# Attention, gated convolution and spatial gating on one core: q and k loads with an earliest time, a mask added by TensorE, and bits found by ScalarE

## The chip, the cores and the metric

The kernel runs on one core of a Trainium2 chip. The metric is the device time of one execution in microseconds (us). The times shown are the median of three runs and, beside it, one execution that was profiled.

## What is computed

The reference chains three parts on 4 batches of 576 positions, in float32 at the end:

```python
# q, k, v: (4, 8, 576, 64); window 64, causal
scores = q @ k.T / 8;  mask = (0 <= rel) & (rel < 64)
attn = softmax(where(mask, scores, -1e9)) @ v          # per head, then heads side by side: x (4, 576, 512)
h = relu(x @ w_in)                                     # w_in (512, 1024)
conv = sum over k of conv_w[k] * h shifted by k - 1    # 3 taps along the positions
y = (h * sigmoid(conv)) @ w_out                        # w_out (1024, 512)
h2 = relu(y @ w2_in); u, v2 = the halves of h2
vn = layer norm of v2;  vs = w_spatial @ vn + b        # mixes the positions
out = (u * vs) @ w2_out
```

The matrices of weights come as 64-bit floats; the kernel reads them as pairs of 32-bit words and makes 32-bit floats of them by integer operations.

## The kernel before, in words

**Attention.** The 36 blocks of 64 queries are taken in pairs, 18 rounds in all (`rec_round`, p = 0 to 17). A round multiplies q with k for both blocks and all heads into two PSUM tiles s, one per head half (L537, 32 products). VectorE adds the mask and takes the row's extreme in one fused instruction per head pair (L553, four per half), writing masked scores into the SBUF tile sm. ScalarE takes exponentials in place with the sum beside them (L562, eight per round), then follow the reciprocal (L570, L571), the normalisation (L578 on ScalarE or L582), transposes by TensorE (L592), copies to pts, the products with v (L618) and the split of the result into a rounded high part and a low part (xc, L285 and L306). The tag s has two buffers and vw, the values, three.

**Loads.** Batch 0's q and k come in five pieces (`rec_load_first`, L454) that TensorE transposes (L489). Batches 1 to 3 come in eight loads each, four of q and four of k (`rec_load_qk`, L466), in pieces of 128 bytes, which VectorE then transposes in blocks of 32 (L503). Values come by L477. All go through one queue, SyncE's, in the order of the list.

**Weights.** `rec_conv` loads one 128x512 tile of 64-bit words (raw, two buffers), scales the high words (L285, wt), takes the low words' upper bits (u1, `low_bits`, L410) and the sign (u2, `sign_bits`, L416) and joins them (u3, L422). 28 such tiles are converted: eight of w_in, eight of w_out, eight of w2_in, four of w2_out. Then each is split into a high and a low part.

**Stage 1** takes the positions in eight chunks of 288 (two a batch). Chunk 0 needs rounds 0 to 2, chunk 1 rounds 3 and 4. `rec_g1` makes one block of 128 columns of h: 12 products of 128x290 (L710 to L712), relu (L301), three taps (L733, L738), tanh (L749), gate (L753) and a split. `rec_g2` makes y (L777 to L779) and stores it to DRAM (L802). **Stage 2** loads y again and makes v, u, the spatial mixing (L1053 to L1059), the gate (L1067, L1070) and the last products (L1106 to L1108).

**What sets the order.** The kernel records operations with a rank, the engines that may do them, their cost, and what they read, write and hold (`Plan.op`). `Plan.emit` then plays them through as a list scheduler and writes out the instructions in the order in which it started them; each engine works through its own in that order. A free engine takes the ready operation of the lowest rank. Where several engines may do one, it takes the one with the least of its waiting work and cost times a bias: by planner time t the bias is BIAS1 below TE1, BIAS2 below TE2, BIAS after that; ScalarE's is 1. The loads are operations on the planner's engine "D": the queue is held 0.45 (ISSUE) for each, the wires for their cost, and the next can be issued without a look at the wires. An operation is ready once all it reads is there and the buffer that it takes over is free; the queue isn't held idle for a rank that lies far ahead.

The ranks come from the constants of PLAN: TA is the rank of round 0, TR the step of the first three rounds, TL and T_G make the chunks' starts, RD and LEAD place the later rounds, QL and QL1 the loads of q and k before their round, VL those of the values, WI, WIS, WO, WOS and W2 the weights, LD a load before its conversion.

Of the kernel before, what the change touches and what calls it, by code (L numbers as in the profile page):

```python
# [15 lines left out]
PSUM = bass.MemoryType.PSUM  # L16
NEG = -8.0e9
BIG = 3.0e38
EXP_SHIFT = 2.0 ** -112

PLAN = {
    "BP": 2.148,
    "BP1": 0.05,
    "BP2": 15.503,
    "BV": 0.462,
    "BV1": 0.753,
    "BV2": 4.229,
    "CS": 2.842,
    "CW": 4.897,
    "CWL": -1.999,  # L30
    "DC": 1.72,
    "G2": 7.85,
    "LAT": 0.209,
    "LD": 0.07,
    "LEAD": -0.623,
    "PORT": 1.851,
    "QK": 0.74,
    "QL": -0.201,
    "QL1": -1.324,
    "QV": -0.054,  # L40
    "RD": 5.317,
    "RS": 1.023,
    "SW": 4.365,
    "TA": -1.408,
    "TE1": 1.82,
    "TE2": 574.465,
    "TL": 1.208,
    "TR": 0.83,
    "VL": -0.489,
    "W2": 13.512,  # L50
    "WI": 1.844,
    "WIS": -0.265,
    "WO": -0.591,
    "WOS": 2.232,
}
LAT = PLAN["LAT"]
HOLD, ISSUE = 0.25, 0.45
BIAS = {"V": PLAN["BV"], "P": PLAN["BP"]}
# [26 lines left out]
class Plan:  # L85
# [4 lines left out]
    def __init__(self):  # L90
        self.rows, self.bufs, self.ops = {}, [], []
        self.writer, self.readers = {}, {}
        self.port, self.issues = set(), {}

    def buf(self, key, n, make):
        return Buf(self, key, n, make)

    def op(self, rank, engs, fn, r=(), w=(), b=(), after=(), port=False, issues=1):


        i = len(self.ops)
        if port:
            self.port.add(i)
        self.issues[i] = issues
        deps = set(after)
# [12 lines left out]
        for x in b:  # L118
            x.users.append(i)
        deps.discard(i)  # L120
        self.ops.append([rank, engs, fn, deps, b])
        return i

    def emit(self):
# [19 lines left out]
        for i in range(n):  # L144
            if not left[i]:
                heapq.heappush(events, (0.0, 0, i))
        port_free = wire = 0.0
        order = []
        t = 0.0
        while events:  # L150
            t = events[0][0]
            while events and events[0][0] <= t + 1e-9:
                _, kind, i = heapq.heappop(events)
                if kind == 0:
                    rank, opt = ops[i][0], ops[i][1]
# [12 lines left out]
            for e in engs:  # L168
                while ready[e] and free[e] <= t + 1e-9:
# [44 lines left out]
def tile_attention_convglu_spatial(  # L214
# [46 lines left out]
    ident = const.tile([P, P], F, name="ident")  # L261
    masks = [const.tile([P, P], F, name=f"mask{j}") for j in range(3)]
    cw = const.tile([P, 3, KF], F, name="cw")
# [91 lines left out]
    def setup_masks(e):  # L355


        for mk_, first in zip(masks, ((False, False), (True, False), (False, True))):
            for h in range(2):
# [15 lines left out]
    op(-9.0, {"A": 1.6}, setup_table, w=["zero1"])  # L375
    op(-8.0, {"P": 3.0}, setup_masks, w=["masks"])

# [29 lines left out]

    def low_bits(u, raw):
# [51 lines left out]
    def rec_load_qk(b, rank):  # L460

        for nm, src, dst in (("q", q, qT), ("k", k, kT)):
            for g in range(4):
                def ld(e, src=src, dst=dst, g=g):
# [44 lines left out]
    def x_pieces(blocks):  # L509
# [10 lines left out]
        return out_  # L520

    x_keys = {qc: [] for qc in range(NQ)}

    def rec_round(p, rank):
# [5 lines left out]
        st = mk(at, [P, 3, 2, HP], F, "st", "st", 3)  # L530

        def mm_s(e):
# [9 lines left out]
        op(  # L542
            rank, {"T": 1.1}, mm_s,
            r=[("q", b, i) for b, i in blocks] + [("k", b, k0 + o) for (b, _), k0 in zip(blocks, k0s) for o in range(2)],
            w=[("s", p, h) for h in range(2)], b=pss + [qT[b] for b in bs] + [kT[b] for b in bs],
        )
        firsts = [i == 0 for _, i in blocks]
        mask = masks[1 if firsts[0] else 2 if firsts[1] else 0]
# [45 lines left out]
        for h in range(2):  # L594
            op(rank + 1 * rs + 0.1 * h, {"V": 1.46}, mx(h), r=[("s", p, h), "masks"], w=[("sm", p, h)], b=[pss[h], sm[h], st])
            op(rank + 2 * rs + 0.1 * h, {"A": 1.9}, ex(h), r=[("sm", p, h)], w=[("ex", p, h)], b=[sm[h], st])
            if p < first_rounds:
# [42 lines left out]
    def rec_conv(rank, load, n, issues=1, lead=PLAN["LD"]):  # L640
# [14 lines left out]
        def u1(e):  # L655
            low_bits(u(), raw())

# [541 lines left out]
```

## Time and profile before

| | us |
|---|---|
| median of 3 runs | 548.48 (547.16 to 550.54) |
| profiled execution, its own time | 549.49 |
| its span, first to last instruction | 547.7 |
| TensorE busy in the span | 508.4 |
| VectorE, ScalarE, GpSimd busy | 345.1, 324.4, 4.3 |
| mean granted clock of TensorE (1.0 is 2.4 GHz) | 0.956 |

The span is what the trace covers; the profiled execution's own time has 1.8 us around it. A start in a timeline counts from the span's start. Instructions of one engine overlap a little in the trace, so the time from one start to the next tells what an instruction costs its engine. In the timeline of SyncE's queue the second number is the time that the issue took, for as many transfers as "x" says. The DMA share is the mean busy share of 16 engines and can pass 1 where packets overlap.

### The profile page before, as it was taken

The page shows a single profiled execution, that of the slowest core. Times are in us where ns is not written, and L with a number is a line of the kernel's source. Part 1 is how long each engine was busy: PE and PEld are TensorE (multiplying, and loading weights), DVE is VectorE, ACT ScalarE, POOL GpSimd, SP SyncE. Part 2 cuts the span into 40 slices and gives each one's busy share as a digit, 9 for nine tenths or more (in the row PEclk, how much of TensorE's full clock was granted, in tenths as well). Part 3 has the DMA queues.
Part 4 walks back from the last instruction along what each step waited for, and adds up shares of the span by engine and source line. Part 5 has one row for each costly group of instructions (what it writes and reads, how often), then busy time and mean ns, then how long its engine had stood idle before and what let it go on. Part 6 is the DMA issues. An engine that isn't in the chain of part 4 may idle for free.

```text
span 547.7 us, 11063 instructions
## 1 busy us (share of the span) xinstructions
PE 508.4 (93%) x4198; PEld 472.7 (86%) x4198; DVE 345.1 (63%) x1045; ACT 324.4 (59%) x920; POOL 4.3 (1%) x34
## 2 busy tenths in 40 slices
PE   5745967999999999999999999999999999999997
PEld 5634857899988999999999998898899889988996
DVE  2547768999977989777676634986506740572160
ACT  4875879988959899678785524653322442233221
POOL 3000000000000000000000000000000000000000
PEclk9765788999998999999999999999999999999999
DMA  9999997655996746224216682560105011202003
GB/s 181 173 145 178 147 184 209 190 162 148 208 151 183 226 117 181 68 61 143 69 45 196 215 303 93 166 208 4 59 20 172 1 63 35 87 1 78 1 0 97
DMA packets 131993, 68.05 MB, mean 124 GB/s; under 512 B 105740, under 2 KB 118308, under 8 KB 131940
## 3 DMA queue, kind: packets, MB, share of 16 engines
q1 hardware_dynamic: 131940, 67.35, 51.5%
q8 instruction: 33, 0.54, 0.4%
q14 instruction: 20, 0.16, 0.1%
HBM read 48.98 MB, written 18.35 MB: 123 GB/s over the span
## 4 chain that ended last, share of the span: by engine, by line
PE 80%; DMA 7%; SPq 5%; ACT 3%; DVE 3%; issue 1%; ACTq 0%
PE y L777 6%; PE h L710 5%; PE h L711 5%; PE y L779 5%; PE h L712 5%; PE y L778 5%; DMA vw<-in_v_dram 3%; PE pv L618 3%; PE sps L1053 3%; PE sps L1055 3%; PE sps L1054 3%; PE ops L1108 3%; PE vps L930 3%; PE ops L1107 3%; PE ops L1106 3%; PE vps L929 3%
## 5 line engine op out<-in xcount | busy, mean ns | idle before, releaser
L710 PE MATMUL h<-xc,wi 128*128 128x290 f32 x256 | 79.7, 311 | 2.1 <-ACT hs L301 2.1
L777 PE MATMUL y<-g,wo 128*128 128x288 f32 x256 | 78.4, 306 | 0.8 <-DVE ys L795 0.8
L712 PE MATMUL h<-xc,wi 128*128 128x290 f32 x256 | 77.2, 301 | 0.0
L711 PE MATMUL h<-xc,wi 128*128 128x290 f32 x256 | 77.1, 301 | 0.0
L779 PE MATMUL y<-g,wo 128*128 128x288 f32 x256 | 76.1, 297 | 0.0
L778 PE MATMUL y<-g,wo 128*128 128x288 f32 x256 | 75.9, 296 | 0.0
L738 DVE SCALAR_TENSOR_TENSOR cv<-hs,cw,cv 128x288 f32<-128x288 f32 x128 | 64.5, 512 | 15.9 <-ACT cv L733 14.7
L1067 DVE TENSOR_TENSOR gr<-sps,bb 128x288 f32<-128x288 f32 x32 | 14.5, 454 | 71.9 <-PE sps L1059 71.9
L562 ACT ACTIVATE sm<-sm,st 128x128 f32<-128x128 f32 x144 | 55.7, 391 | 2.2 <-DVE st L553 2.2
L710 PEld LDWEIGHTS h<-xc,wi 128*128 128x128 f32 x256 | 49.9, 195 | 3.8 <-ACT hs L301 2.9
L777 PEld LDWEIGHTS y<-g,wo 128*128 128x128 f32 x256 | 48.5, 189 | 2.7 <-DVE ys L795 1.1
L711 PEld LDWEIGHTS h<-xc,wi 128*128 128x128 f32 x256 | 49.9, 195 | 0.0
L712 PEld LDWEIGHTS h<-xc,wi 128*128 128x128 f32 x256 | 49.6, 194 | 0.1
L779 PEld LDWEIGHTS y<-g,wo 128*128 128x128 f32 x256 | 48.7, 190 | 0.0
L778 PEld LDWEIGHTS y<-g,wo 128*128 128x128 f32 x256 | 48.6, 190 | 0.0
L578 ACT ACTIVATE sm<-sm,st 128x128 f32<-128x128 f32 x132 | 41.1, 393 | 1.0 <-DVE st L571 0.8
L285 ACT ACTIVATE gd<-gr 128x288 fp32r<-128x288 f32 (+1 forms) x32 | 13.4, 418 | 47.2 <-DVE gr L1070 47.2
L553 DVE CUSTOM_DVE_ANT_0 sm<-s,mask 128x128 f32<-128x128 f32 x144 | 32.3, 286 | 10.9 <-PE s L537 10.9
L989 PE MATMUL ups<-yt,w2i 128*128 128x288 f32 x128 | 37.9, 296 | 0.0
L990 PE MATMUL ups<-yt,w2i 128*128 128x288 f32 x128 | 37.9, 296 | 0.0
L991 PE MATMUL ups<-yt,w2i 128*128 128x288 f32 x128 | 37.9, 296 | 0.0
L618 PE MATMUL pv<-pts,vw 128*64 128x64 f32 x576 | 25.8, 250 | 12.5 <-DMA vw<-in_v_dram 9.4
(147 smaller groups left out, 1240.5 us busy)
## 6 DMA issues: line engine op xcount, KB each, us to landing
yd<-ys SPq DMA_DIRECT2D x32, 288.0 KB, 3.0
yt<-yd SPq DMA_DIRECT2D x32, 288.0 KB, 4.3
vw<-in_v_dram SPq DMA_DIRECT2D x32, 256.0 KB, 4.0
raw<-in_moe_w_out_dram SPq DMA_DIRECT2D x12, 512.0 KB, 3.9
raw<-in_moe_w_in_dram SPq DMA_DIRECT2D x16, 256.0 KB, 5.3
raw<-in_moe_w_in_dram SPq DMA_DIRECT2D x8, 512.0 KB, 5.0
w2i<-w2d SPq DMA_DIRECT2D x8, 512.0 KB, 6.1
out_dram<-osb SPq DMA_DIRECT2D x15, 256.0 KB, 2.0
```

The source lines that it names most:

```text
L562: nc.scalar.activation(out=sm[h]()[:, hp, :], in_=sm[h]()[:, hp, :], func=ACTF.Exp, scale=-1.0, bias=st()[:, 0, h, hp:hp + 1], accum_out=s ...
L578: nc.scalar.activation(out=sm[h]()[:, hp, :], in_=sm[h]()[:, hp, :], func=ACTF.Copy, scale=st()[:, 2, h, hp:hp + 1])
L618: mm(psv()[h * W:h * W + W, hp, j * W:j * W + W], vas[j]()[:, hp + HP * h, :], pts[h]()[:, hp, j * W:j * W + W], start=True, stop=True,)
L710: mm(hps(), wh, xh, start=(kk == 0), stop=False)
L711: mm(hps(), wh, xl, start=False, stop=False)
L712: mm(hps(), wl, xh, start=False, stop=(kk == KD - 1))
L738: return lambda e: nc.vector.scalar_tensor_tensor(out=cv(), in0=h[:, o + j:o + j + CH], scalar=cw[:, j, f:f + 1], in1=cv(), op0=ALU.mult, ...
L777: mm(yps(), wt[:, 0], gt[:, 0, :], start=(kk == 0), stop=False)
L778: mm(yps(), wt[:, 0], gt[:, 1, :], start=False, stop=False)
L779: mm(yps(), wt[:, 1], gt[:, 0, :], start=False, stop=(kk == KF - 1))
L989: mm(ups(), wt[:, 0], yt[b][0]()[:, kk, o], start=(kk == 0), stop=False)
L990: mm(ups(), wt[:, 0], yt[b][1]()[:, kk, o], start=False, stop=False)
```

## The change

1. Loads of q and k of batches 1 to 3 get an earliest planner time, `at`, equal to their rank, and a cost of 2.5 in place of 1.8. In the planner a DMA queue now also stays taken until the wires are no more than DEPTH = 6 behind, and ISSUE is 0.5.
2. In rounds 0 to 5 TensorE puts the mask into both score tiles first: a product of the identity and the mask, 128 columns by 512, in fp32r, and the scores are added to it in PSUM. VectorE then takes the maximum of a half in one reduction and multiplies it by -1/8 in a small second instruction; the exponentials read the scores from PSUM. So the score tiles are held until the exponentials are done, and sm is first written by these. The masks are built in a tile of tag wu and copied, with the identity, to fp32r tiles by VectorE (`put_masks`). NEG becomes -2**33.
3. u1 of `rec_conv` may go to VectorE (at 0.05 more) or to ScalarE (at its cost of a 128x512 instruction from SBUF): a copy with scale 2**-13 and bias 2**-14 - 0.5 that writes 16-bit integers.
4. All constants of PLAN but BP1, DC and LAT change, among them the biases: for VectorE 0.753, 4.229, 0.462 become 3.844, 3.449, 1.729 and for GpSimd 0.05, 15.503, 2.148 become 0.05, 3.023, 0.615, and TE2, from which on the last of the three holds, 574.465 becomes 183.169. So any operation may change its place in the order, and some their engine.

```diff
-NEG = -8.0e9
+NEG = -(2.0 ** 33)
...
-    "LEAD": -0.623,
+    "LEAD": 1.709,
-    "QL": -0.201,
-    "QL1": -1.324,
+    "QL": -0.104,
+    "QL1": -4.718,
-    "RD": 5.317,
+    "RD": 1.962,
-    "TA": -1.408,
-    "TE1": 1.82,
-    "TE2": 574.465,
-    "TL": 1.208,
-    "TR": 0.83,
-    "VL": -0.489,
-    "W2": 13.512,
-    "WI": 1.844,
-    "WIS": -0.265,
-    "WO": -0.591,
-    "WOS": 2.232,
+    "TA": -0.261,
+    "TE1": 1.949,
+    "TE2": 183.169,
+    "TL": 0.206,
+    "TR": 6.98,
+    "VL": -18.824,
+    "W2": 83.412,
+    "WI": 0.394,
+    "WIS": -7.725,
+    "WO": 0.771,
+    "WOS": 1.466,
...
-HOLD, ISSUE = 0.25, 0.45
+HOLD, ISSUE, DEPTH = 0.25, 0.5, 6.0
...
-                heapq.heappush(events, (0.0, 0, i))
+                heapq.heappush(events, (max(0.0, self.at.get(i, 0.0)), 0, i))
...
-                            heapq.heappush(events, (t, 0, j))
+                            heapq.heappush(events, (max(t, self.at.get(j, 0.0)), 0, j))
...
-                        free[e] = t + ISSUE * self.issues[i]
+                        free[e] = max(t + ISSUE * self.issues[i], wire - DEPTH)
...
+    mf = mk(p2, [P, 3, P], F, "wu", "mf", 1)
+
+    def put_masks(e):
+        for j in range(3):
+            nc.vector.tensor_copy(out=masks_r[j], in_=mf()[:, j])
+        nc.vector.tensor_copy(out=ident_r, in_=ident)
+    op(-8.0, {"P": 3.0}, setup_masks, w=["masks_f"], b=[mf])
+    op(-7.0, {"V": 0.6}, put_masks, r=["masks_f", "ident"], w=["masks", "masks_r"], b=[mf])
...
+        if e == "A":
+            nc.scalar.activation(
+                out=halves(u)[:, :, 0], in_=halves(raw.rearrange("p c w -> p (c w)"))[:, 0::2, 1],
+                func=ACTF.Copy, scale=2.0 ** -13, bias=2.0 ** -14 - 0.5,
+            )
+            return
...
-                op(rank + 0.1 * g, {"D": 1.8}, ld, w=[(nm, b, "ld", g)], b=[dst[b]])
+                op(rank + 0.1 * g, {"D": 2.5}, ld, w=[(nm, b, "ld", g)], b=[dst[b]], at=rank)
...
+    EARLY = 6
...
+            if early:
+                for h in range(2):
+                    mm(pss[h](), ident_r, masks_r[which].unsqueeze(1).to_broadcast([P, HP, P]), start=True, stop=False)
...
-                            kT[b]()[rows, hp, k0s[j] * W:k0s[j] * W + P], start=True, stop=True,
+                            kT[b]()[rows, hp, k0s[j] * W:k0s[j] * W + P], start=not early,
+                            stop=not early or hp == HP - 1,
...
+                if early:
+                    m = st()[:, 0, h]
+                    nc.vector.tensor_reduce(out=m, in_=pss[h](), axis=mybir.AxisListType.X, op=ALU.max)
+                    nc.vector.tensor_scalar(out=m, in0=m, scalar1=-scale, scalar2=None, op0=ALU.mult)
+                    return
...
+                    src = pss[h] if early else sm[h]
                     nc.scalar.activation(
-                        out=sm[h]()[:, hp, :], in_=sm[h]()[:, hp, :], func=ACTF.Exp, scale=-1.0,
+                        out=sm[h]()[:, hp, :], in_=src()[:, hp, :], func=ACTF.Exp, scale=scale if early else -1.0,
...
+                r=[("sm", p, h)], w=[("ex", p, h)], b=[sm[h], st] + [pss[h]] * early,
...
-        op(rank, {"V": c_ts(n)}, u1, r=[(key, "raw")], w=[(key, "u1")], b=[raw, u], port=True)
+        op(rank, {"V": c_ts(n) + 0.05, "A": c_act(n, False)}, u1, r=[(key, "raw")], w=[(key, "u1")], b=[raw, u], port=True)
```

## Rows read from the trace of the kernel before

**Rows 1.** Page, section 1: busy us (share of the span) xinstructions, each engine

```profile
PE 508.4 (93%) x4198; PEld 472.7 (86%) x4198; DVE 345.1 (63%) x1045; ACT 324.4 (59%) x920; POOL 4.3 (1%) x34
```

**Rows 2.** View of stretches: stretch, length, busy us of each engine, clock, DMA share, GB/s

```profile
7.00:57.10 50.10, 28.03 (x326) 21.94 (x325) 28.27 (x128) 36.27 (x125) 0.00 (x0) 0.66 1.15 173
0.00:57.10 57.10, 33.66 (x353) 27.57 (x354) 29.10 (x133) 37.76 (x127) 4.34 (x34) 0.71 1.09 170
57.10:88.60 31.50, 23.75 (x258) 21.94 (x256) 23.56 (x77) 26.15 (x83) 0.00 (x0) 0.83 1.08 174
88.60:117.00 28.40, 26.31 (x241) 24.63 (x234) 27.80 (x59) 25.43 (x63) 0.00 (x0) 1.00 0.65 191
117.00:544.50 427.50, 424.72 (x3357) 398.59 (x3356) 264.67 (x778) 234.66 (x651) 0.00 (x0) 1.00 0.39 110
```

**Rows 3.** Timeline of TensorE: start us, us, what, [idle before <-releaser]

```profile
43.96 0.66 PE L489 MATMUL tr<-ident,qk 64*128 64x64 f32 x4 [2.78 <-DMA qk<-in_q_dram]
...
53.35 1.76 PE L618 MATMUL pv<-pts,vw 128*64 128x64 f32 x28 [0.72 <-DMA vw<-in_v_dram]
...
57.15 0.59 PE L710 MATMUL h<-xc,wi 128*128 128x290 f32 x1
...
88.66 0.40 PE L710 MATMUL h<-xc,wi 128*128 128x290 f32 x1
```

**Rows 4.** Timeline of SyncE's queue: start us, us in the queue's issue, what

```profile
17.66 1.41 SPq L466 DMA_DIRECT2D qT<-in_q_dram  x1
...
27.11 2.92 SPq L676 DMA_DIRECT2D raw<-in_moe_w_in_dram  x2
30.07 0.60 SPq L466 DMA_DIRECT2D qT<-in_q_dram  x1
...
39.04 2.85 SPq L454 DMA_DIRECT2D qk<-in_q_dram  x2
...
46.03 4.42 SPq L477 DMA_DIRECT2D vw<-in_v_dram  x3
...
52.34 0.60 SPq L466 DMA_DIRECT2D qT<-in_q_dram  x1
...
66.13 2.58 SPq L676 DMA_DIRECT2D raw<-in_moe_w_in_dram  x2
...
70.04 2.80 SPq L466 DMA_DIRECT2D qT<-in_q_dram  x1
...
75.72 2.17 SPq L676 DMA_DIRECT2D raw<-in_moe_w_in_dram  x2
```

**Rows 5.** Timeline of VectorE, same columns

```profile
18.86 0.29 DVE L553 CUSTOM_DVE_ANT_0 sm<-s,mask 128x128 f32<-128x128 f32 x1 [3.31 <-PE s L537]
...
20.55 0.46 DVE L410 TENSOR_SCALAR wu<-raw 128x512 uint16<-128x512 uint16 x1
20.90 0.45 DVE L416 TENSOR_SCALAR wu<-raw 128x512 uint16<-128x512 uint16 x1
...
36.83 0.68 DVE L306 TENSOR_TENSOR xc<-pv,xc 128x512 fp32r<-128x512 f32 x1
37.45 0.29 DVE L553 CUSTOM_DVE_ANT_0 sm<-s,mask 128x128 f32<-128x128 f32 x1
```

**Rows 6.** Timeline of ScalarE

```profile
21.01 0.67 ACT L285 ACTIVATE wt<-raw 128x512 f32<-128x512 f32 x1
21.58 0.39 ACT L562 ACTIVATE sm<-sm,st 128x128 f32<-128x128 f32 x1
...
24.66 0.57 ACT L285 ACTIVATE qT<-tr 128x512 f32<-128x512 f32 x1
```

**Rows 7.** Timeline of TensorE in the last stage

```profile
534.00 0.40 PE L1107 MATMUL ops<-w2o,gd 128*128 128x512 f32 x1
534.24 0.39 PE L1108 MATMUL ops<-w2o,gd 128*128 128x512 f32 x1
```

**Rows 8.** Timeline of GpSimd

```profile
1.02 0.29 POOL masks.py:199 TENSOR_SCALAR_AFFINE_SELECT ident<-ident 128x128 f32<-128x128 f32 x1
```

More of the change, by code (lines that the diff above doesn't have):

```diff
@@ L21 @@
 PLAN = {
-    "BP": 2.148,
+    "BP": 0.615,
     "BP1": 0.05,
[L24 to L30, printed above, removed]
+    "BP2": 3.023,
+    "BV": 1.729,
+    "BV1": 3.844,
+    "BV2": 3.449,
+    "CS": 2.677,
+    "CW": -2.142,
+    "CWL": 0.708,
     "DC": 1.72,
-    "G2": 7.85,
+    "G2": 7.067,
     "LAT": 0.209,
-    "LD": 0.07,
-    "LEAD": -0.623,
-    "PORT": 1.851,
-    "QK": 0.74,
-    "QL": -0.201,
-    "QL1": -1.324,
-    "QV": -0.054,
-    "RD": 5.317,
-    "RS": 1.023,
-    "SW": 4.365,
-    "TA": -1.408,
-    "TE1": 1.82,
-    "TE2": 574.465,
-    "TL": 1.208,
-    "TR": 0.83,
-    "VL": -0.489,
-    "W2": 13.512,
-    "WI": 1.844,
-    "WIS": -0.265,
-    "WO": -0.591,
-    "WOS": 2.232,
+    "LD": -0.554,
+    "LEAD": 1.709,
+    "PORT": 0.519,
+    "QK": 0.218,
+    "QL": -0.104,
+    "QL1": -4.718,
+    "QV": -0.674,
+    "RD": 1.962,
+    "RS": 2.062,
+    "SW": 1.562,
+    "TA": -0.261,
[9 more added lines that the diff above has]
+    "WOS": 1.466,
 }
 LAT = PLAN["LAT"]
-HOLD, ISSUE = 0.25, 0.45
+HOLD, ISSUE, DEPTH = 0.25, 0.5, 6.0
 BIAS = {"V": PLAN["BV"], "P": PLAN["BP"]}
@@ L92, in __init__, with op @@
         self.writer, self.readers = {}, {}
-        self.port, self.issues = set(), {}
+        self.port, self.issues, self.at = set(), {}, {}
     def buf(self, key, n, make):
         return Buf(self, key, n, make)
-    def op(self, rank, engs, fn, r=(), w=(), b=(), after=(), port=False, issues=1):
+    def op(self, rank, engs, fn, r=(), w=(), b=(), after=(), port=False, issues=1, at=0.0):
         i = len(self.ops)
@@ L104, in op @@
         self.issues[i] = issues
+        self.at[i] = at
         deps = set(after)
@@ L261, in tile_attention_convglu_spatial @@
     ident = const.tile([P, P], F, name="ident")
-    masks = [const.tile([P, P], F, name=f"mask{j}") for j in range(3)]
+    masks_r = [const.tile([P, P], R, name=f"mask{j}") for j in range(3)]
+    masks = [x_.bitcast(F) for x_ in masks_r]
+    ident_r = const.tile([P, P], R, name="ident_r")
     cw = const.tile([P, 3, KF], F, name="cw")
@@ L355, in setup_masks @@
     def setup_masks(e):
-        for mk_, first in zip(masks, ((False, False), (True, False), (False, True))):
+        for mk_, first in zip([mf()[:, j] for j in range(3)], ((False, False), (True, False), (False, True))):
             for h in range(2):
@@ L375, in tile_attention_convglu_spatial @@
     op(-9.0, {"A": 1.6}, setup_table, w=["zero1"])
-    op(-8.0, {"P": 3.0}, setup_masks, w=["masks"])
+    mf = mk(p2, [P, 3, P], F, "wu", "mf", 1)
[5 more added lines that the diff above has]
+    op(-7.0, {"V": 0.6}, put_masks, r=["masks_f", "ident"], w=["masks", "masks_r"], b=[mf])
     def setup_ones(e):
@@ L406, in halves, with low_bits @@
         return x_.bitcast(H16).rearrange("p (c w) -> p c w", w=2)
-    def low_bits(u, raw):
+    def low_bits(u, raw, e="V"):
+        if e == "A":
[4 more added lines that the diff above has]
+            return
         nc.vector.tensor_scalar(
@@ L530, in rec_round @@
         st = mk(at, [P, 3, 2, HP], F, "st", "st", 3)
+        firsts = [i == 0 for _, i in blocks]
+        which = 1 if firsts[0] else 2 if firsts[1] else 0
+        mask = masks[which]
+        early = p < EARLY
         def mm_s(e):
+            if early:
+                for h in range(2):
+                    mm(pss[h](), ident_r, masks_r[which].unsqueeze(1).to_broadcast([P, HP, P]), start=True, stop=False)
             for hp in range(HP):
@@ L542, in rec_round @@
         op(
-            rank, {"T": 1.1}, mm_s,
-            r=[("q", b, i) for b, i in blocks] + [("k", b, k0 + o) for (b, _), k0 in zip(blocks, k0s) for o in range(2)],
+            rank, {"T": 1.75 if early else 1.1}, mm_s,
+            r=["masks_r"] * early + [("q", b, i) for b, i in blocks] + [("k", b, k0 + o) for (b, _), k0 in zip(blocks, k0s) for o in range(2)],
             w=[("s", p, h) for h in range(2)], b=pss + [qT[b] for b in bs] + [kT[b] for b in bs],
         )
-        firsts = [i == 0 for _, i in blocks]
-        mask = masks[1 if firsts[0] else 2 if firsts[1] else 0]
         def mx(h):
             def f(e):
+                if early:
[3 more added lines that the diff above has]
+                    return
                 for hp in range(HP):
@@ L594, in rec_round @@
         for h in range(2):
-            op(rank + 1 * rs + 0.1 * h, {"V": 1.46}, mx(h), r=[("s", p, h), "masks"], w=[("sm", p, h)], b=[pss[h], sm[h], st])
-            op(rank + 2 * rs + 0.1 * h, {"A": 1.9}, ex(h), r=[("sm", p, h)], w=[("ex", p, h)], b=[sm[h], st])
+            kept = [sm[h], st] if not early else [st]
+            op(
+                rank + 1 * rs + 0.1 * h, {"V": 0.85 if early else 1.46}, mx(h),
+                r=[("s", p, h), "masks"], w=[("sm", p, h)], b=[pss[h]] + kept,
+            )
+            op(
+                rank + 2 * rs + 0.1 * h, {"A": 1.75 if early else 1.9}, ex(h),
+                r=[("sm", p, h)], w=[("ex", p, h)], b=[sm[h], st] + [pss[h]] * early,
+            )
             if p < first_rounds:
@@ L655, in u1 @@
         def u1(e):
-            low_bits(u(), raw())
+            low_bits(u(), raw(), e)
         def u2(e):
```

## The prediction

> **What bounds the kernel now.** I read the page's busy shares first: TensorE is busy 508.4 of 547.7 us [rows 1], so at most 39 us of standing still can go, and whatever a slow clock costs, and the question is where they lie. The stretches of the span answer it [rows 2]. From 117 to 544.5 us TensorE works 424.7 of 427.5 us at granted clock 1.00 (2.4 GHz), and 3.2 us remain behind its last product: that part gives back no more than 2.8 us. The loss lies ahead. Up to 57.1 us TensorE is busy 33.7 us at a mean clock of 0.71 (1.0 is 2.4 GHz, 0.5 is 1.2), up to 88.6 us 23.8 of 31.5 at 0.83, and from there to 117 us 26.3 of 28.4 at 1.00. Counted at the full level, busy time times clock, the first two stretches hold 23.9 and 19.7 us of work, so 33 and 12 us are lost there, by waiting and by the slow clock.
>
> What TensorE waits for is in its order of time [rows 3]: the last piece of batch 0's q (to 43.96), values of the third round (to 53.35), and only then the first product of stage 1 at 57.15; the eighth block of stage 1 begins at 88.66. Both waits end with a transfer, so next comes the order of SyncE's queue [rows 4]. It starts eight loads of batch 1 from 17.66 to 27.11 and from 30.07 to 39.04, 9.4 and 9.0 us, and only behind them the last piece of batch 0 (39.04) and the values of round three (46.03). Eight loads of batch 2 follow, six from 52.34 to 66.13 and two from 70.04 to 75.72, 19.5 us, ahead of the last block of w_in. One such load holds the queue 2.3 us; the DMA share of 1.09 and 1.08 [rows 2] says that the wires are full, so that is transfer and not issue alone. VectorE and ScalarE are the limit behind that: ScalarE is busy 37.8 of the first 57.1 us, and from 88.6 to 117 VectorE is busy 27.8 of 28.4.
>
> **The loads held back.** In the old list nothing keeps batch 1 and 2 from being planned as soon as the planner's queue is free; there a load costs it 0.45 us, so it sees no jam. Now they have an earliest planner time. By the new constants I work out 27.2 for batch 1, 91.1 for batch 2 and 134.9 for batch 3 (the rank of their first round plus 0.1). Batch 0's last piece has no such time; ahead of it by rank stand eight other q and k loads, one of conv_w, two of w_in and three of v, 17.1 units of wire, which with the new limit of 6 are issued by about 11. So it passes batch 1, and so do the values of round three once their buffers are free. This gives the order, not a time. In time the row of 39.04 moves up by at most 18.4 us. ScalarE bounds it from the other side: from 57.1 us it can give back only what it stood idle, 57.1 - 37.8 = 19.3, of which 5.5 lie ahead of 7.1 us, before the first data have been transposed; 13.8 remain, the row from 7.0 us. Below, nothing is gained if another wait steps in. I take 13, near ScalarE's bound, because new ranks also let rounds that stage 1 doesn't need yet fall behind.
>
> From 57.1 to 88.6 batch 2's 19.5 us leave the queue, but batch 1's 18.4 come into it. ScalarE stood idle 5.4 us there and VectorE 7.9 [rows 2]; between nothing and 5.4 I take 3. What arrives earlier meets a full VectorE from 88.6 on, with the conversion of w_out. The bounds are no loss and the whole 3 just won; I take 2 given back. Behind the held loads stand stores of y and loads of v, in the one queue; batch 2's 19.5 us now fall where the DMA share was 0.65 or less, so I take nothing, with 4 us as the other end (two waits of 2 us, against 2.8 us of idle in all from 117).
>
> **Mask by TensorE.** Six rounds have 12 more products of 128 columns by 512. Such a product starts every 0.24 us at the full clock [rows 7], 0.48 at half of it: 2.8 to 5.8 us. The first three rounds lie ahead of stage 1, where TensorE waits anyway; the other six products are 1.4 us in its stream, of which I count 1. If that cover is gone, all 5.8 count. The four fused instructions of a half go: eight took 18.86 to 20.55, 0.85 a half [rows 5]. In their place stand a maximum over 512 elements from PSUM, for which the nearest row is the difference that starts 0.62 before the next [rows 5], and a small multiplication; that is a gain of 0.1 or a loss of 0.2 a half, so -1.2 to +2.4 for 12, taken as zero. Four copies of masks and identity join VectorE's start; at the 0.62 of the same row they are 2.5 us at most, and end while the first q is still on its way. The exponentials now read PSUM; their eight took 3.08 us a round [rows 6] and I leave them so. But they now hold the two score buffers, which the maximum used to set free: see the slower rival.
>
> **Upper bits by ScalarE.** Up to 28 weight tiles can move. VectorE is rid of 0.35 us each (the next instruction starts so much later, [rows 5]), ScalarE gets one like its copy of a 128x512 raw tile, 0.57 [rows 6]. For the eight of w_in this is 2.8 off VectorE and 4.6 on ScalarE, which is the fuller of the two up to 88.6. Behind that VectorE is the fuller (27.8 against 25.4), and the move helps. Between -2.8 and +4.6 I take +1.5. The planner charges VectorE 3.4 times the cost up to planner time 183, so most will go to ScalarE.
>
> The Trainium skill speaks against this part: ScalarE: Activation LUTs, section "Rules for kernel authors", gives multiply and add to VectorE and not to ScalarE. The rows agree on the price of one, but not on what it does here, since it relieves the engine that is full from 88.6 us on. By the rule alone the whole 4.6 would count, and the sum would end 3.1 us later.
>
> **GpSimd.** From planner time 183 the constants make GpSimd the cheapest place for products and differences in SBUF. The trace has no such instruction; its select of 128x128 took 0.29 us [rows 8], by length 0.65 for 288 elements; below lies nothing gained or lost, above a chain that lengthens by 0.65 at the last product, where TensorE waits. TensorE is the limit there with 2.8 us of idle in 427, so I take zero.
>
> **Sum.** -13 - 3 + 2 + 1 + 1.5 = -11.5 us. The profiled execution took 549.5 us (span 547.7 and 1.8 around it), the median is 548.5; so 538.0 for one like the profiled one and 537.0 for the median.
>
> **Rivals.**
> A. The vector engines keep the head as it is: the transfers come earlier, but ScalarE and VectorE, 53 and 64 us busy in the first 88.6, are filled by conversions in another order, and stage 1 starts only 6 us sooner. -6 + 1 + 1.5 = -3.5: 545. For it: the waits of TensorE on ScalarE in the same stretch. Against: ScalarE's gaps end with transfers of w_in.
> B. The head shrinks as far as the queue allows: -18.4 - 5.4 + 2 + 1 = -20.8, so 527.5. For it: the queue is the only thing that put 39.04 and 46.03 so late. Against: it needs ScalarE's early rounds in another order and nearly without a gap.
> C. Slower: the score buffers. Scores of a round now wait for the last exponential of the round before, and TensorE runs in order, so stage 1 stands behind them. A round needs 0.85 us of maximum and 3.08 of exponentials behind its scores, some 4 us; where the list puts two rounds closer, TensorE waits up to 3.08. In five of the six rounds that is 15 us. With the moved bits and masks at their upper ends: -13 - 3 + 2 + 5.8 + 4.6 + 15 = +11 at the worst and, with the masks hidden, +6: 554. It decides from early rounds less than 4 us apart. Against: the list knows of these buffers, and stage 1 lies between later rounds.
> D. The hold doesn't do what it says: if the planner's clock runs ahead of the chip by more than some 15 us, batch 1 still stands ahead of what round three needs. Then only batch 2 moves: -3 + 2 + 1 + 1.5, 550.
>
> **How the numbers follow.** Forecast (531 to 542) 0.55; A 0.15, half of it above 543; B 0.12; C 0.12; D 0.06. What can be told from no change is about 1%, 5.5 us, so the bounds are 543 and 554. A measures as same in half its cases, D in nearly all; C is slower in three quarters: faster 0.745, same 0.165, slower 0.09. The range from 526 to 551 holds the forecast, A, D and most of B; C and the far end of B, under 2 in 10, are left out.
>
> **What would show it.** Right: in SyncE's order batch 1 begins only behind the values of round three, stage 1 starts near 44 us and its eighth block near 73, and the stretch that is full of TensorE begins 11 to 12 us sooner and is no longer than it was. Wrong: a wait of scores on exponentials in PE's waits (C); ScalarE without gaps to 57 us and stage 1 not before 50 (A); stage 1 before 40 (B); batch 1 ahead of 39.04's piece (D); or waits above 3 us in all behind the start of the full stretch, with stores of y behind batch 2.

## The result, and the profile after

The changed kernel takes 533.34 us (median of four executions, 532.93 to 533.38) against 548.30 (median of four) for the kernel before on the same chip: a ratio of 0.972 [0.969, 0.975]. Forecast were 537.0 in a range from 526 to 551. The profiled execution took 533.38 us, with a span of 531.5 in place of 547.7. The busy shares come first, from the page, as in [rows 1]:

```profile
PE 508.5 (96%) x4210; PEld 472.5 (89%) x4210; DVE 346.3 (65%) x935; ACT 314.2 (59%) x889; POOL 74.1 (14%) x95
```

TensorE is busy as long as before. What went is time in which it stood still: 39 us of the span were left over before and 23 are now. The view of stretches (stretch, length, busy us of PE, PEld, DVE, ACT, POOL with their counts, granted clock, DMA share, GB/s), cut where stage 1 begins, at its eighth block, and where TensorE's full stretch begins, answers to [rows 2]:

```profile
0.00:44.70 44.70, 31.93 (x321) 25.14 (x321) 23.95 (x67) 31.64 (x111) 4.34 (x34) 0.76 1.00 178
44.70:67.60 22.90, 19.42 (x158) 17.84 (x158) 19.00 (x38) 19.15 (x44) 0.00 (x0) 0.80 1.06 183
67.60:105.20 37.60, 34.15 (x323) 31.73 (x320) 35.39 (x91) 36.92 (x116) 0.00 (x0) 0.91 0.72 177
105.20:528.30 423.10, 422.93 (x3413) 397.75 (x3413) 267.96 (x742) 226.08 (x620) 69.72 (x61) 1.00 0.43 116
```

Busy time times clock gives the work at the full level, and the length less that is what a stretch loses to waits and to the slow clock. After, the four lose 20.4, 7.4, 6.5 and 0.2 us, 34.5 in all; the four of [rows 2] from 0 on lost 33.2, 11.8, 2.1 and 2.8, 49.9 in all. The work itself is 494.6 before and 493.8 after. So the 15.4 us less that are lost are nearly the whole of the 16.2 by which the span is shorter, and no work of TensorE was saved. The measure is rough, because the clock is a mean over each stretch: the twelve new products, some 2.9 us at the full clock, don't show in it.

TensorE's timeline has the same landmarks as [rows 3] (start, us, what, idle before and releaser):

```profile
33.81 0.79 PE L560 MATMUL s<-mask,ident_r 128*128 128x512 f32 x1 [0.69 <-ACT sm L594]
...
44.75 0.61 PE L749 MATMUL h<-xc,wi 128*128 128x290 f32 x1 [0.37 <-ACT xc L290]
...
63.00 1.50 PE L565 MATMUL s<-kT,qT 64*64 64x128 f32 x30 [2.34 <-DVE kT L522]
...
67.64 0.61 PE L749 MATMUL h<-xc,wi 128*128 128x290 f32 x1
...
77.27 1.75 PE L657 MATMUL pv<-pts,vw 128*64 128x64 f32 x30 [1.54 <-ACT pts L290]
...
80.87 0.43 PE L749 MATMUL h<-xc,wi 128*128 128x290 f32 x1
```

Stage 1 begins at 44.75, not 57.15, and its eighth block at 67.64, not 88.66. The scores of round 4 (63.00) now stand late in chunk 0's blocks, and that round's values at 77.27, behind the eighth block. SyncE's queue, as in [rows 4], shows why (start, us in the issue, what). Stage 1 needs the third round (round 2, as rounds are counted from 0), and the third round needs the fourth and the fifth load of values (25.30, not shown, and 32.21):

```profile
21.18 1.27 SPq L473 DMA_DIRECT2D qk<-in_k_dram  x2
...
32.21 0.37 SPq L496 DMA_DIRECT2D vw<-in_v_dram  x1
32.63 0.58 SPq L485 DMA_DIRECT2D qT<-in_q_dram  x1
...
38.41 2.73 SPq L715 DMA_DIRECT2D raw<-in_moe_w_in_dram  x2
...
52.11 2.31 SPq L485 DMA_DIRECT2D kT<-in_k_dram  x1
54.53 2.94 SPq L715 DMA_DIRECT2D raw<-in_moe_w_in_dram  x2
...
95.49 0.42 SPq L485 DMA_DIRECT2D qT<-in_q_dram  x1
```

Batch 0's last piece of q and k is issued by 22.5, the fifth load of values by 32.6, and only then begins batch 1, from 32.63 to 54.4 with w_in between its loads. Batch 2 begins at 95.49; before, that was 52.34.

### The profile page after: what moved, and what is told of

Read it like the earlier page. It is cut to its first block, busy times and chain, and to the rows that moved or that the text cites. A ratio compares the mean times of both kernels' runs of the same rounds, so it can differ in the third digit from the quotient of the medians.

```text
span 531.5 us, 11111 instructions
## 1 busy us (share of the span) xinstructions
PE 508.5 (96%) x4210; PEld 472.5 (89%) x4210; DVE 346.3 (65%) x935; ACT 314.2 (59%) x889; POOL 74.1 (14%) x95
## 4 chain that ended last, share of the span: by engine, by line
PE 83%; ACT 10%; DMA 3%; DVE 2%; issue 1%; POOL 0%; SPq 0%; ACTq 0%; POOLq 0%
PE h L749 6%; PE h L750 6%; PE y L816 6%; PE h L751 6%; PE y L818 5%; PE y L817 5%; PE sps L1092 3%; PE sps L1094 3%; PE sps L1093 3%; PE ops L1147 3%; PE vps L968 3%; PE ops L1145 3%; PE vps L969 3%; PE ops L1146 3%; PE pv L657 3%; PE vps L967 3%
## 5 line engine op out<-in xcount | busy, mean ns | idle before, releaser
L777 DVE SCALAR_TENSOR_TENSOR cv<-hs,cw,cv 128x288 f32<-128x288 f32 x128 | 68.8, 549 | 15.2 <-ACT cv L772 14.6
L1106 DVE TENSOR_TENSOR gr<-sps,bb 128x288 f32<-128x288 f32 x32 | 14.6, 457 | 81.5 <-PE sps L1098 80.7
L311 POOL TENSOR_TENSOR g<-cv,g 128x576 fp32r<-128x576 f32 x16 | 24.5, 1529 | 200.0 <-ACT g L290 183.2
L749 PEld LDWEIGHTS h<-xc,wi 128*128 128x128 f32 x256 | 49.9, 195 | 2.4 <-issue 0.7
L751 PEld LDWEIGHTS h<-xc,wi 128*128 128x128 f32 x256 | 49.9, 195 | 0.0
L1109 POOL TENSOR_TENSOR gr<-gr,ut 128x288 f32<-128x288 f32 x31 | 26.6, 858 | 141.5 <-DVE gr L1106 137.7
L290 ACT ACTIVATE gd<-gr 128x224 fp32r<-128x224 f32 (+1 forms) x31 | 12.9, 417 | 44.8 <-POOL gr L1109 44.7
L1030 PE MATMUL ups<-yt,w2i 128*128 128x288 f32 x128 | 37.8, 296 | 0.0
L594 ACT ACTIVATE sm<-sm,st 128x128 f32<-128x128 f32 x96 | 37.3, 400 | 0.0
L610 ACT ACTIVATE sm<-sm,st 128x128 f32<-128x128 f32 x116 | 35.9, 398 | 1.5 <-DVE st L603 1.1
```

The source lines that it names most:

```text
L594: nc.scalar.activation(out=sm[h]()[:, hp, :], in_=src()[:, hp, :], func=ACTF.Exp, scale=scale if early else -1.0, bias=st()[:, 0, h, hp:hp ...
L610: nc.scalar.activation(out=sm[h]()[:, hp, :], in_=sm[h]()[:, hp, :], func=ACTF.Copy, scale=st()[:, 2, h, hp:hp + 1])
L749: mm(hps(), wh, xh, start=(kk == 0), stop=False)
L751: mm(hps(), wl, xh, start=False, stop=(kk == KD - 1))
L777: return lambda e: nc.vector.scalar_tensor_tensor(out=cv(), in0=h[:, o + j:o + j + CH], scalar=cw[:, j, f:f + 1], in1=cv(), op0=ALU.mult, ...
L1030: mm(ups(), wt[:, 1], yt[b][0]()[:, kk, o], start=False, stop=(kk == KD - 1))
```

## The experiments

In those called "order kept" the list is the changed kernel's, and only the named instructions move or change their engine. In those called "replanned" the scheduler runs again with the altered costs, so that anything may move. Before any of them ran, two theories stood. By the one, the held loads bring the gain, and the moves between engines are worth little either way. By the other, it is those moves and the new constants that bring it. Neither came out as it stands.

**Each held batch taken up again, order kept.** In `f1_batch1_early` batch 1's eight loads go back ahead of batch 0's last piece; in `f2_batch2_early` batch 2's go behind the scores of round 4, where they stood from 64.41 to 80.7, ahead of tiles of w_out.

```diff
 # in Plan.emit, before the instructions are written out
+ahead = set(self.held[1])                      # f2: self.held[2]
+moved = [o for o in order if o[2] in ahead]
+order = [o for o in order if o[2] not in ahead]
+k = [o[2] for o in order].index(self.first[4, 0])   # f2: index(self.scores[4]) + 1
+order[k:k] = moved
```

> The changed kernel with its own order kept on every engine, and only batch 1's eight loads of q and k taken up in SyncE's queue, to stand ahead of the last piece of batch 0, as they stood in the kernel before. Theory (the hold of batch 1 is what brings stage 1 forward): the last piece and the third round's values come some 18 us later, stage 1 starts at 57 to 62 us in place of 44.8, and the time rises by 8 to 14 us, to 541 to 547. Rival (the new constants, the mask and the bits carry the gain, and the queue had room): stage 1 starts within 3 us of where it did and the time rises by 0 to 3 us.

> The changed kernel with its own order kept, and only batch 2's eight loads taken up in SyncE's queue, to the first place where their buffers are free by the list (behind the scores of round 4), ahead of the next values and w_out. Theory (the second hold is worth something of its own): values and w_out come up to 18 us later while TensorE already needs them; the full stretch begins later and the time rises by 4 to 12 us, to 537 to 545. Rival (between 60 and 90 us the wires are free for a fourth of the time and VectorE and ScalarE set the pace): the time rises by less than 2 us.

Measured: 551.81 us, a ratio of 1.005 [1.003, 1.007] to before, and 549.85, 1.002 [1.000, 1.005]. Either one gives back the whole gain, more than was expected of it. Timelines of `f1_batch1_early`, the queue and TensorE:

```profile
18.90 1.12 SPq L491 DMA_DIRECT2D qT<-in_q_dram  x1
...
34.05 2.50 SPq L491 DMA_DIRECT2D kT<-in_k_dram  x1
36.59 3.05 SPq L479 DMA_DIRECT2D qk<-in_q_dram  x2
...
43.07 0.66 PE L516 MATMUL tr<-ident,qk 64*128 64x64 f32 x4 [19.01 <-DMA qk<-in_k_dram]
```

Eight loads from 18.90 to 36.6 are one wait of 19.0 us, and stage 1 begins at 62.96, 18.2 later; the time is 18.5 longer. Of `f2_batch2_early`, ScalarE and TensorE:

```profile
87.17 0.67 ACT L296 ACTIVATE wt<-raw 128x512 f32<-128x512 f32 x1 [16.47 <-DMA raw<-in_moe_w_out_dram]
...
88.81 1.35 PE L632 MATMUL pt<-ident,sm 128*128 128x128 f32 x4 [15.95 <-ACT sm L618]
```

Here stage 1 (44.84) and the eighth block (68.16) are where the change puts them. ScalarE then stands 16.5 us before a conversion of w_out, in its fixed order; the normalisation of a round's weights (L618), which TensorE needs, is behind that. 16.0 us of wait are 16.5 in the time. The loss was expected too small because the list was planned for the held loads, so nothing in it fills the hole.

**No hold, replanned.** `r_no_hold` leaves the new constants and both moves and gives the loads their old terms.

```diff
-HOLD, ISSUE, DEPTH = 0.25, 0.5, 6.0
+HOLD, ISSUE, DEPTH = 0.25, 0.45, 1.0e9
-op(rank + 0.1 * g, {"D": 2.5}, ld, ..., at=rank)
+op(rank + 0.1 * g, {"D": 1.8}, ld, ...)
```

> The changed kernel planned anew without the hold: no earliest time, no limit on how far the wires may be behind, the old costs of a load (0.45 and 1.8), but all new constants, the mask by TensorE and the bits by ScalarE. Theory: the constants and the two moves of work gain little without the hold: 544 to 556. Rival (they carry the gain): 533 to 538.

Measured: 555.19 us, 1.011 [1.007, 1.015], stage 1 at 53.08 and the eighth block at 89.42. Without the hold the rest of the change is a loss; with it the same constants and moves take 21.9 us less.

**The hold alone, replanned.** `r_before_hold` is the kernel before with `at`, DEPTH, ISSUE 0.5 and the cost of 2.5, and nothing else.

```diff
-HOLD, ISSUE = 0.25, 0.45
+HOLD, ISSUE, DEPTH = 0.25, 0.5, 6.0
... (in Plan.emit: at, and the limit DEPTH, as in the change)
-op(rank + 0.1 * g, {"D": 1.8}, ld, ...)
+op(rank + 0.1 * g, {"D": 2.5}, ld, ..., at=rank)
```

> The kernel before planned anew with the hold alone: earliest times, the limit on the wires, the new costs of a load; its old constants, its mask by VectorE and its bits by VectorE. Theory: most of the gain comes with it, though the constants were not made for it: 535 to 542. Rival: within 3 us of 548.

Measured: 545.98 us, 0.995 [0.992, 0.998]: 2 to 3 us of the 15, as the rival had it. The head is better (stage 1 at 51.72, the eighth block at 73.93), and then it is given back. Two stretches of it, columns as above:

```profile
80.00:100.00 20.00, 17.65 (x162) 16.37 (x163) 19.17 (x42) 17.98 (x44) 0.00 (x0) 0.91 0.50 145
100.00:120.00 20.00, 16.24 (x128) 14.80 (x127) 18.46 (x52) 16.56 (x49) 0.00 (x0) 0.91 1.26 173
```

And the same two of the changed kernel:

```profile
80.00:100.00 20.00, 19.97 (x184) 19.17 (x177) 18.60 (x51) 19.77 (x52) 0.00 (x0) 0.98 0.67 184
100.00:120.00 20.00, 19.74 (x197) 19.04 (x196) 18.48 (x55) 19.93 (x63) 0.00 (x0) 1.00 1.26 176
```

VectorE is as full in both, but TensorE stands still for 6.1 of 40 us in the one and for 0.3 in the other, and its clock falls with it. With the old constants the full stretch of TensorE does not begin by 120.

This is not the hold of the change, though. The earliest time of a load is its rank, and the rank comes from the constants: worked out as the prediction did for the new ones, the old ones give 14.4, 95.0 and 152.3 for batches 1 to 3, where the new ones give 27.2, 91.1 and 134.9. So batch 1 is held 13 planner us less. In the queue its first load is issued at 22.73, and seven of its eight stand ahead of the third round's fifth load of values (42.82). TensorE waits for values twice ahead of stage 1, 3.5 us and 2.8. What the run shows is that a hold with the old times does little.

**Old constants, replanned.** `r_old_constants` is the changed kernel, its hold and both moves kept, with all of PLAN as before.

```diff
 PLAN = {
-    ... (the changed kernel's constants)
+    ... (the constants of before)
```

> The changed kernel planned anew with all 36 constants of the kernel before, and the hold, the mask by TensorE and the bits by ScalarE kept. The hold alone with the old constants gave 546. Theory (the gain hangs on the order as a whole; the two moves of work are worth 1 to 1.5 us each where the order is kept): 540 to 547, that is 7 us or more above the changed kernel. Rival (the moves carry what the hold alone left): 533 to 538.

Measured: 543.37 us, 0.991 [0.988, 0.994]; stage 1 at 57.39, the eighth block at 75.76. 10 of the 15 us are missing without the new constants. Here too batch 1 is held only to 14.4. All eight of its loads stand ahead of the fifth load of values (46.98), and TensorE stands still for it:

```profile
52.63 1.76 PE L657 MATMUL pv<-pts,vw 128*64 128x64 f32 x28 [8.64 <-DMA vw<-in_v_dram]
```

**One constant, replanned.** `r_w2_old` puts back W2 alone, the step in rank from one weight tile of stage 2 to the next, which moved furthest of the constants that make ranks.

```diff
-    "W2": 83.412,
+    "W2": 13.512,
```

> The changed kernel planned anew with one constant of before, W2 (the step in rank from one tile of w2_in to the next, 13.5 in place of 83.4), so that w2_in is converted earlier. Theory (between 80 and 130 us VectorE and ScalarE are full, and what stands there of w2_in's conversions delays TensorE): 535 to 541. Rival (the order is robust to it): 532.5 to 534.5.

Measured: 533.93 us, 0.973 [0.968, 0.978]: the gain doesn't hang on this one.

**Mask and bits back on VectorE, order kept.** `mask_vector` takes out the twelve products and the reduction, and VectorE adds the mask in all rounds; `u1_vector` finds all upper bits on VectorE.

```diff
 # mask_vector
-if early:                      # the products of identity and mask
+if False:
-start=not early, stop=not early or hp == HP - 1
+start=True, stop=True
-if early:                      # reduction and small multiply
+if False:
-src = pss[h] if early else sm[h]
+src = sm[h]
-func=ACTF.Exp, scale=scale if early else -1.0
+func=ACTF.Exp, scale=-1.0
 # u1_vector
-low_bits(u(), raw(), e)
+low_bits(u(), raw(), "V")
```

> The changed kernel with its own order kept, and the mask of the first six rounds added by VectorE again in the four fused instructions of a half, the exponentials reading SBUF. Theory (the mask by TensorE is worth no more than some 1 us): 532 to 535. Rival (it is what frees ScalarE and VectorE ahead of stage 1): stage 1 starts 2 us later or more and the time is 536 or more. Second rival (holding the score buffers costs): 531 or less.

> The changed kernel with its own order kept, and the upper bits of all 28 weight tiles found by VectorE again (23 of them were on ScalarE). VectorE is full from 60 to 100 us, where some 8 of these stand at 0.35 us each. Theory: the move gives what VectorE is rid of there, so undoing it costs 1 to 3 us: 534 to 536. Rival (ScalarE has the tighter place, at 0.64 us each): it gains 1 to 3 us, 530 to 532.

Measured: 535.09 us, 0.975 [0.972, 0.977], and 534.80, 0.974 [0.971, 0.977]. Stage 1 begins at 45.1 and 43.73. Undoing either costs nothing that its interval tells from the change's. By the medians it is 1.8 and 1.5 us, and the shortest executions (534.78 and 533.63) are longer than the longest of the changed kernel (533.38); but the kernel before, run beside them, was slower as well (549.37), so a worth of 1 to 2 us is likely and not shown.

**GpSimd.** `no_gpsimd` gives the 61 products and differences that the list put on GpSimd to VectorE; `gpsimd_head` gives GpSimd the low parts of w_out's eight tiles as well, from 70 to 100 us. Order kept in both.

```diff
 # no_gpsimd
-ops[i][2](e)
+ops[i][2]("V" if e == "P" and "V" in ops[i][1] else e)
 # gpsimd_head
-ops[i][2](e)
+ops[i][2]("P" if i in self.wo_low else e)
```

> The changed kernel with its own order kept, and every product and difference that GpSimd took given to VectorE (61 of them, 70 us of GpSimd, some 35 of VectorE), all behind 120 us. Theory (TensorE is the limit there): within 1.5 us of 533. Rival (GpSimd's share is what removed the 2.8 us of waits behind 117 us): 535 to 537.

> The changed kernel with its own order kept, and the eight differences that make w_out's low parts, which VectorE does between 72 and 100 us at 0.6 us each, given to GpSimd, which is idle there. Theory (VectorE is the limit there, and an idle engine relieves it): 529 to 532. Rival (while GpSimd works on a pair of tiles VectorE's instructions in SBUF wait for it: the conversions of the changed kernel took up to 1.9 us, where 0.69 is usual, once GpSimd worked; and the low part comes 0.8 us later): 534 to 540.

Measured: 533.20 us, 0.971 [0.969, 0.974], and 535.88, 0.977 [0.972, 0.982]. So GpSimd's share, 70 of its 74 us, is worth nothing where it lies, and more of it early on is no help.

**The new constants, planned with the old work.** `r_constants` keeps hold and constants, but the scheduler has mask and bits on VectorE.

```diff
-    EARLY = 6
+    EARLY = 0
-op(rank, {"V": c_ts(n) + 0.05, "A": c_act(n, False)}, u1, ...)
+op(rank, {"V": c_ts(n)}, u1, ...)
```

> Planned anew with the hold and all new constants, but the mask and the bits by VectorE as before. The hold alone with the old constants gave 546. Theory (the constants that place the work around the hold give the rest): 533 to 538. Rival (the two moves to TensorE and ScalarE give it): 542 to 547.

Measured: 550.28 us, 1.002 [1.000, 1.004], the plainest miss of the study. Its timeline of TensorE:

```profile
46.07 0.68 PE L565 MATMUL s<-kT,qT 64*64 64x128 f32 x2
58.63 2.15 PE L565 MATMUL s<-kT,qT 64*64 64x128 f32 x30 [11.88 <-DVE kT L522]
60.71 1.97 PE L657 MATMUL pv<-pts,vw 128*64 128x64 f32 x32
...
63.07 0.40 PE L749 MATMUL h<-xc,wi 128*128 128x290 f32 x1 [0.38 <-ACT xc L290]
```

The scores of round 4 stand ahead of stage 1 here, and they need batch 1's k, which the hold has made late. TensorE waits 11.9 us for it, with the third round's products (60.71) and all of stage 1 behind it. In the changed kernel the same scores are at 63.00, behind most of chunk 0's blocks. But these scores aren't what makes stage 1 late. The queue shows it, from batch 1's first load on:

```profile
29.74 0.60 SPq L485 DMA_DIRECT2D qT<-in_q_dram  x1
...
49.92 2.34 SPq L485 DMA_DIRECT2D kT<-in_k_dram  x1
...
55.13 0.54 SPq L496 DMA_DIRECT2D vw<-in_v_dram  x1
```

All eight loads of batch 1 stand ahead of the fifth load of values, which takes 5.6 us to land, to 60.7: just when the scores are through. Without the scores the third round's products would have had to wait till then all the same. It is the wait of rival D, batch 1 ahead of what round three needs, in a list with the full hold.

The planner decides this by a hair. Played through from the text of both kernels, on its own clock, it has the following. The buffer for the fifth load of values comes free at 26.9 in the changed kernel, and the load is issued there, 0.3 ahead of batch 1's earliest time of 27.2. In `r_constants` the products that free the buffer are planned 0.3 later. The queue is then taken by a tile of w_in, and when it is free, at 28.0, batch 1 has the lower rank (27.2 against 32.5); the load follows at 47.2. The other planned costs that come with mask and bits are enough for that.

**The order alone.** That leaves work and order to be told apart. `old_work` keeps the changed kernel's order and has mask and bits on VectorE, as `r_constants` has, and nothing of the list on GpSimd. There the two differ: the list of `r_constants` gives GpSimd 68 products and differences, one of them (at 29.57) ahead of stage 1. `no_gpsimd` measured such a share as worth nothing in the changed kernel's order; in the order of `r_constants` that wasn't tried.

```diff
 # the edits of mask_vector, u1_vector and no_gpsimd together
```

> The changed kernel's own order on every engine, but all work as it was before: mask and upper bits by VectorE, nothing on GpSimd behind the masks. What is left of the change is the order alone, the held loads in it. Singly the three undone moves cost 1.5, 1.0 and nothing. Theory (they add up, and the order carries the rest of the gain): 534.5 to 537.5, so 11 to 14 us of the 15. Rival (VectorE, full from 60 to 100 us, can't take all three back): 539 or more.

Measured: 535.01 us, 0.973 [0.969, 0.977], with these stretches:

```profile
0.00:44.00 44.00, 27.62 (x314) 22.76 (x314) 25.65 (x119) 30.48 (x107) 4.34 (x34) 0.80 0.99 182
44.00:66.70 22.70, 19.05 (x157) 17.70 (x157) 19.30 (x46) 16.54 (x39) 0.00 (x0) 0.80 1.05 175
66.70:100.00 33.30, 29.65 (x282) 27.55 (x281) 33.23 (x105) 30.05 (x98) 0.00 (x0) 0.84 0.65 181
100.00:529.20 429.20, 427.85 (x3451) 402.53 (x3449) 279.99 (x824) 225.36 (x626) 0.00 (x0) 1.00 0.45 116
```

The landmarks are those of the change: stage 1 at 43.97, the eighth block at 66.66. The three moves of work together have no worth in this order that the intervals tell, 0.973 against 0.972; by the medians it is 1.7 us. Nearly the same work in the order of `r_constants` is 15 us slower. What the change brings is its order, and the moves bring that the scheduler, which counts their costs, finds it.

What in the order? In this table the first number is how many of batch 1's eight loads the queue issues ahead of the fifth load of values; then come the starts in us of the third round's products (the last group of them) and of stage 1, and the median.

| | batch 1 ahead | third round's products | stage 1 | median |
|---|---|---|---|---|
| before | 8 | 53.35 | 57.15 | 548.30 |
| changed kernel | 0 | 42.41 | 44.75 | 533.34 |
| `r_w2_old` | 0 | 42.59 | 44.33 | 533.93 |
| `old_work` | 0 | 42.25 | 43.97 | 535.01 |
| `r_before_hold` | 7 | 49.57 | 51.72 | 545.98 |
| `r_no_hold` | 8 | 50.94 | 53.08 | 555.19 |
| `r_old_constants` | 8 | 52.63 | 57.39 | 543.37 |
| `r_constants` | 8 | 60.71 | 63.07 | 550.28 |

Stage 1 is early in those lists alone in which the values pass batch 1. In the other lists the products end a wait for their values, but for `r_constants`, where the scores hide that wait. In the kernel before and in `r_no_hold` batch 0's last piece stands behind batch 1 too. The time doesn't follow stage 1 alone: what a list does behind it counts too, as `r_no_hold` and `f2_batch2_early` show.

What isn't settled: no run moved the fifth load of values alone, so its share of the 15 us is read from the traces. And which of the many constants make this order is open: W2 alone was shown not to, and the biases, TR, VL and WIS were not taken one by one.

## Why the prediction was right, and where its terms were off

**Loads held back, -13 up to stage 1: right.** 57.15 became 44.75, -12.4. `f1_batch1_early` shows the mechanism as it was told, a queue in which batch 1 stands ahead of batch 0's last piece. ScalarE, taken as the limit, is busy 31.6 of the 44.7 us, against 37.8 of 57.1: half of the 12.4 is work that no longer lies ahead of stage 1 and half is idle time, of which 13.1 are left of 19.3. So the bound that I chose came close without being the limit. There is luck in the step as well. I let the values of round three pass batch 1 "once their buffers are free" and didn't work out when that is; in the planner it is 0.3 us before it would have been too late, and in `r_constants` it fails.

**-3 up to the eighth block: too small.** That stretch went from 31.5 to 22.9 us, -8.6, outside the bound of 5.4 that I drew from ScalarE's idle time. The bound took the work in the stretch as given. The new list moves round 4's values and the conversions around them behind the eighth block (77.27; the next block of h comes only at 80.87). ScalarE is busy 19.2 us there instead of 26.2. TensorE has 158 products there and not 258; by busy time times clock, 4.2 of the 8.6 us are work that went behind the stretch, and 4.4 are lost time, inside the bound. So the landmark flatters: the ninth block begins at 80.87 where it was 90.36, 9.5 us sooner and not 21. An engine's idle time bounds what a stretch can give only while the stretch keeps its work.

**+2 given back, +1 for the masks, +1.5 for the bits: not to be had one by one.** From the eighth block to the end it is 463.9 us against 459.0, +4.8 where the three sum to +4.5, but that is luck: by the same measure it is 3.0 of moved work, 4.4 more lost up to 105.2, and 2.6 less behind that. The two prices for masks and bits fell: each undone alone gains nothing, and by the medians loses 1.8 and 1.5 us. The steps behind them were near. Eight of the twelve products lie ahead of stage 1, two at 59.67 ahead of the wait of 2.34 at 63.00, and two at 70.73, ahead of waits of 1.6 and 1.5 us: TensorE waits there anyway. A half's maximum and its small multiply cost VectorE 0.79 against 0.85, from its timeline:

```profile
28.75 0.68 DVE L580 TENSOR_REDUCE st<-s 128x4 f32<-128x512 f32 x1
29.46 0.17 DVE L581 TENSOR_SCALAR st<-st 128x4 f32<-128x4 f32 x1
29.54 0.69 DVE L441 SCALAR_TENSOR_TENSOR wt<-wt,wu 128x512 int32<-128x512 int32 x1
```

For the bits, 23 of 28 tiles went to ScalarE, at 0.64 from start to start where I had 0.57, from ScalarE's timeline:

```profile
18.91 0.77 ACT L424 ACTIVATE wu<-raw 128x512 uint16<-128x512 uint16 x1
19.54 0.35 ACT L594 ACTIVATE sm<-s,st 128x128 f32<-128x128 f32 x1
...
19.87 0.37 ACT L594 ACTIVATE sm<-s,st 128x128 f32<-128x128 f32 x1
```

The Trainium skill's rule (ScalarE: Activation LUTs, "Rules for kernel authors") gives such work to VectorE, and by the prediction's working it would have added 3.1 us here. The trace agrees with it on the price, 0.64 against the 0.35 of VectorE in [rows 5]; `u1_vector`, which follows it, is not faster.

**Nothing for the waits behind the full stretch: wrong by 2.6.** I kept the 2.8 us of idle behind 117 us [rows 2] and gave room for 4 more. After, 0.2 are left from 105.2 on. Late loads of batch 2 and 3 and the stores of y didn't collide. What took the waits away no run shows by itself; it isn't GpSimd's share, since `no_gpsimd` is no slower.

**The sum: 4.7 us short, nearly all in one stretch.** The span is 16.2 us shorter and the sum had 11.5. By stretches that is 0.6 too much up to stage 1, 5.6 too little up to the eighth block, and 0.3 too little for what comes back. The signs came out but for one: batch 1 behind the values, stage 1 at 44.75 for 44, the full stretch 11.8 us sooner and 4.4 shorter; the eighth block was forecast near 73 and came at 67.64.

**GpSimd, zero: right**, though not by its bound. I took 0.65 us for 288 elements from a select of 0.29 for 128. The groups of lines (busy us, mean ns) say:

```profile
L1109 POOL TENSOR_TENSOR gr<-gr,ut 128x288 f32<-128x288 f32 x31 | 26.6, 858 | 141.5 <-DVE gr L1106 137.7 <-DVE lst L986 3.8
```

0.86 us, in a stage where TensorE has its work ready.

**The rivals.** C: the one wait of scores on exponentials is the 0.69 at 33.81, not 15. A: stage 1 moved 12.4, not 6. D: batch 1 begins behind the values. B did not happen for stage 1, but its larger second term was nearer than mine. (Two slips, without weight: in A the busy times stand in the wrong order, 53 us are VectorE's and 64 ScalarE's, and B's sum is 527.7.) What I had not among the rivals was the order itself. The hold, so clearly the cause in the queue, brings only 2 to 3 us with the earliest times of the old constants, and the list of `r_constants`, with the full hold, is no faster than before. I took the list as one in which stage 1 and all that it needs pass what is held back; that was so, and it needed the constants and the planned costs to be so.

## What to carry to other kernels

A load issued long before it is needed isn't free when the wires are full: look in the queue's timeline for what stands behind it, and hold it back until that is through. Holding it back pays only if what is urgent then passes it. One load that becomes ready a moment too late stands behind the whole held batch, and one instruction placed too early stops all that its engine has behind it: so read from the queue which load the first late instruction waited for, and what stood ahead of that. To learn whether a change of work or a change of order made the difference, run the old work in the new order.

## What the runs showed of the hardware

VectorE is held up while GpSimd works. In `gpsimd_head`, timelines of GpSimd and of VectorE:

```profile
76.70 1.65 POOL L313 TENSOR_TENSOR wo<-wt,wo 128x512 fp32r<-128x512 f32 x1 [4.73 <-DVE wo L297]
```

```profile
75.52 0.47 DVE L433 TENSOR_SCALAR wu<-raw 128x512 uint16<-128x512 uint16 x1
...
77.25 1.42 DVE L433 TENSOR_SCALAR wu<-raw 128x512 uint16<-128x512 uint16 x1
78.56 0.41 DVE L295 TENSOR_SCALAR wt<-raw 128x512 f32<-128x512 f32 x1
```

The same instruction takes 0.47 us by itself and 1.42 while GpSimd's difference runs, to 78.35: it ends only behind it. In the changed kernel the slowest of each kind on the tile wu (min, median and max ns) show the same: one of 1.69 us at 235.21 and one of 1.92 at 205.04 begin while GpSimd works, from 234.87 to 236.58 and from 204.72 to 206.41, and end behind it:

```profile
L435 DVE TENSOR_SCALAR wu<-raw x28: 420/462/1686, 17.4 to 346.8; 128x512 uint16<-128x512 uint16 x28
L441 DVE SCALAR_TENSOR_TENSOR wt<-wt,wu x28: 640/690/1923, 19.7 to 348.2; 128x512 int32<-128x512 int32 x28
```

The Trainium skill has this as a lock: SBUF — State Buffer, "Who interferes with whom", says that the two engines share a pair of ports, and that where VectorE's instruction needs the pair, the engine that issues second is blocked entirely until the other is done. The 1.42 us agree. What that makes of work given to GpSimd, the busy times tell, of `no_gpsimd` and of `gpsimd_head`:

```profile
PE 506.4 (95%) x4210; PEld 470.5 (88%) x4210; DVE 350.4 (66%) x996; ACT 313.7 (59%) x889; POOL 4.3 (1%) x34
...
PE 506.6 (95%) x4210; PEld 470.5 (88%) x4210; DVE 348.6 (65%) x927; ACT 314.5 (59%) x889; POOL 85.5 (16%) x103
```

In `no_gpsimd` VectorE has 61 instructions more than in the changed kernel, some 35 us by their mean times there (0.45 to 0.75 each), and is busy only 4.1 us longer, 350.4 against 346.3. So of 35 us that moved to GpSimd, VectorE gained 4. In `gpsimd_head` it has eight instructions fewer and is busy 2.3 us longer.

Exponentials that read PSUM were not slower than those from SBUF: one starts 0.33 us behind the other (19.54 to 19.87 above), where eight from SBUF took 3.08 us, 0.385 each, in [rows 6].
